# A transformer block with conditioned layer norms: a new token layout and front end, the second norm turned by transposing DMAs, its modulation folded into W1, and new order seeds

## The chip, the cores and the metric

The kernel runs on one core of a Trainium2 chip. A core has a matrix engine (PE, with PEld for its weight loads), a vector engine (DVE), an activation engine (ACT), a general engine (POOL), and a sync engine (SP) that here issues the DMAs. Matrix products land in PSUM, eight banks of 128x512 fp32; everything else lies in SBUF. The metric is the device time of one execution in microseconds (us). Verdicts compare medians of several executions.

## The reference, cut to what matters

One sequence of S = 2048 tokens, D = 512, 32 heads of 16, an MLP of F = 1376, all bf16. The vector `c` gives six modulation vectors of length 512.

```python
mod = (silu(c) @ w_mod).reshape(1, 6, 1, 512)
sa, ca, ga, sb, cb, gb = mod[:, 0], ..., mod[:, 5]
h = layernorm(x) * (1 + ca) + sa
q, k, v = split_heads(h @ wqkv)                 # 32 heads of 16
p = softmax(q @ k.T * 16 ** -0.5)               # no mask
x = x + ga * ((p @ v) @ wo)
h = layernorm(x) * (1 + cb) + sb
x = x + gb * (gelu(h @ w1 + b1) @ w2 + b2)
```

Nothing in it depends on the order of the tokens, as long as queries, residual and output use one order.

## The kernel before, in words

**A planner writes the order.** The function builds operations (`op`, `chain`, `dma`), each with an engine, an assumed duration, dependencies, a priority and perhaps a buffer to acquire (`Res`). `Plan.step` simulates the engines and commits one operation after another; what it commits is emitted at once, so each engine's instruction stream is fixed in the planner's order. An engine runs its stream in order: an instruction that waits holds all that stand behind it. Where several operations could start at about the same time, `Plan.pick` (line 159) takes the lowest of a priority (`dyn`) plus a small number from `Plan.spread` (line 171). That number is a hash of the operation's kind or of its source line, and of a seed from `SEEDS`, one for each 25 us of planned time. A DMA is assumed to land at the time that lines 245 to 248 work out: its issue, 0.75 us, its size at 260 KB a microsecond, and 0.7 us.

```python
q = "SP"
self.bus[q] = max(self.bus[q], s + o.us + 0.75) + o.kb / (300.0 if s < 12.0 else 260.0)
o.end = self.bus[q] + 0.7
```

**Front.** SP loads the first 512 tokens of x in two halves, then two 512 KB pieces of `w_mod` (`load_mod`, line 537). The first 128 columns of Q, K and V weights and the later x blocks wait for the first of these (`behind`, and `o_wm[0]` as a dependency). `mod_columns` (line 620) makes the first norm's shift and scale, `modA`, by 32 one-column matmuls. `layer_norm` (line 666) does the statistics on DVE (`stats`), the reciprocal root on POOL (`rstd`), the normalised z on DVE (`apply`), the transposes on PE into PSUM, and the modulation from PSUM into h on DVE or ACT (`modulate`, line 652). In the first block column groups 0 and 2 go to DVE, 1 and 3 to ACT; groups 0 and 1 lie in one PSUM tile, 2 and 3 in the other. `proj`, `make_q`, `make_k`, `make_v` (lines 732 to 793) make Q, K and V.

**Attention.** 32 runs of one query block of 512 and four heads each; the last query block's runs hold eight heads on half of the queries. A run has 16 key tiles; a tile is 128 keys by 512 queries for four heads, each head a quarter. Quarters take one of two ways:

- ACT way: scores by L853 into PSUM tiles `st` of three or two banks, exponential by ACT (L926), then PV matmuls (L1038) into `od`.
- DVE way: scores by L853 into one of two banks `ax`, L967 turns them into 16-bit integers `ph`, and four shifts (L987 on DVE, the last sometimes in pieces on POOL, L1003) give four bit patterns that are bf16 approximations. All four are multiplied into `od`, so a DVE tile needs four times as many PV matmuls.

Five key tiles of a run may go the DVE way. `next_tile` gives tiles out as the engines come free, and a tile that DVE does not get goes to ACT. The two banks `ax` serve all other products too: projections, transposes of later blocks, `wo`, W1 and W2. Warming matmuls (L479, L463) fill PE's idle time.

At a run's end `normalise` (line 1061) copies `od` to SBUF (L1063) and turns the denominators through small DMAs (L1069 to L1084), and POOL multiplies (L1090). POOL pieces called `beside` run next to DVE instructions that leave the shared port free.

**Block tails.** When a query block is complete, `block_tail` (line 1241) computes `wo`, adds the residual, normalises (the second layer norm, with `modB`), and does W1, gelu, W2 and the store. Its matmuls get due times spread over the following runs, in steps of a fixed length, and each chain takes one or more steps. The transposes of the second norm go by the `else` branch of `layer_norm` (line 707): eight transposes per `ax` bank, then two modulations on DVE. Three tails have four token tiles; the last block's first half has two, and the remaining two token tiles go through `last_half` (line 1312) once all runs are over. `late_loads` fetches the weights after run 0; after run 3 a chain of kind "gate" makes `modB` and the gates `ga`, `gb`. `w2_scaled` folds gb into W2 and `scaled` folds ga into Wo, on POOL.

Of the kernel before, what the change touches and what calls it, by code (L numbers as in the profile page):

```python
# [11 lines left out]
ACT = mybir.ActivationFunctionType  # L12
ALU = mybir.AluOpType
# [41 lines left out]
PEL = 0.24  # L55
# [11 lines left out]
SEEDS = (133, 8, 244, 706, 635, 613, 830, 607, 557, 981, 249, 97, 553, 633, 53, 586, 376, 469, 873, 940, 563, 742, 976, 448, 82, 180, 131, 20, 555, 353, 321, 992)  # L67
# [43 lines left out]
class Plan:  # L111
# [59 lines left out]
    def spread(self, o):  # L171
        x = ((sum(map(ord, o.kind)) if o.eng == "PE" else o.fn.__code__.co_firstlineno if o.fn else 0) * 2654435761 ^ SEEDS[min(int(self.now // 25.0), len(SEEDS) - 1)] * 2246822519) & 0xFFFFFFFF
        x = ((x ^ x >> 15) * 2246822519) & 0xFFFFFFFF
        return SPREAD * ((x ^ x >> 13) & 1023) / 1024.0
# [107 lines left out]
def kernel(  # L282
# [15 lines left out]
    P = 128  # L298
# [187 lines left out]
    x_src = A_x[0].rearrange("(b t p) d -> b p t d", t=TPB, p=P)  # L486
# [12 lines left out]
    qmask = const.tile([P, 2], FP32, name="qmask")  # L499
    Wo = keep.tile([P, NC, D], BF16, name="Wo")  # L500
# [34 lines left out]
    first = {}  # L535

    def load_mod(i):
        def go(o):
            first[i] = nc.sync.dma_start(out=o.tile, in_=wm_src[:, :, i * D:(i + 1) * D])
        return dma(go, kb=512, acq=r_blk, prio=0.01 + 0.01 * i)  # L540
    o_wm = {i: load_mod(i) for i in (0, 1)}

    def behind(i, load):
        tc.add_manual_dep(load.ins, first[i].ins.name, mybir.DependencyInfo(
            mybir.DependencyClass.Sync, mybir.DependencyReason.DATA), reason="order of loads")
# [4 lines left out]
    def load_cols(i, lo, hi, prio):  # L550
        def go(o):
            got = nc.sync.dma_start(out=o_w[i].tile[:, :, lo:hi], in_=wq_src[:, :, i * D + lo:i * D + hi])
            if lo == 0 and i == 0:
                behind(0, got)
# [65 lines left out]
    def mod_columns(dst, ws, kind, warmer=True):  # L620
        mm = chain([(lambda ps, n=n, w=w, m=m: mod_mm(ps, n, w[1](), m, warmer), 0.36 if warmer else 0.22)
# [9 lines left out]
    o_mA = mod_columns(modA, [(o_wm[i], lambda i=i: o_wm[i].tile, o_wm[i]) for i in range(2)],  # L631
# [34 lines left out]
    def layer_norm(src, deps, mod, mod_dep, hold_z, alloc_h, engines, ps_res, kind, prio,  # L666
# [13 lines left out]
        if isinstance(ps_res, tuple):  # L680
            two = []
            for part in range(2):
                for half in range(2):
                    def tr(o, half=half, part=part):
                        if part:
                            o.tile = two[half].tile
                            two[half].ps = o.tile.bitcast(BF16)
                        ps = o.tile.bitcast(BF16)
                        for j in (2 * half, 2 * half + 1):
                            for t in (2 * part, 2 * part + 1):  # L690
                                nc.tensor.transpose(
                                    out=ps[:, (j % 2) * QB + t * P:(j % 2) * QB + (t + 1) * P],
                                    in_=z.tile[:, t, j * P:(j + 1) * P], identity=ident)
                    one = op("PE", tr, 4 * 0.0705, za[0:2 + 2 * part] + [o_id] + two[half:half + part],
                             lat=PEL, mode=("full", 0), kind=kind,
                             acq=None if part else ps_res[half], rel=(z,))
                    one.use = 0.75
                    two.append(one)
            trs += two[2:4]
            for half in range(2):  # L700
                one, done_tr = two[half], two[2 + half]
                for j in (2 * half, 2 * half + 1):
                    e = engines[j]
                    done.append(op(e, lambda o, j=j, e=e, one=one: modulate(
                        e, h.tile[:, j, :], one.ps[:, (j % 2) * QB:(j % 2 + 1) * QB], mod, j),
                        0.5 if e == "DVE" else 0.72, (done_tr, mod_dep, h), prio=0.2, rel=(one,)))
        else:
            N = nt * P
            per = 2 * QB // N
            for j0 in range(0, NC, per):  # L710
                one = chain([(lambda ps, j=j, j0=j0: [nc.tensor.transpose(
                    out=ps.bitcast(BF16)[:, (j - j0) * N + t * P:(j - j0) * N + (t + 1) * P],
                    in_=z.tile[:, t, j * P:(j + 1) * P], identity=ident) for t in range(nt)], nt * 0.0575)
                    for j in range(j0, j0 + per)], za, kind, r_ax, (z,), per)
                trs.append(one)
                for j in range(j0, j0 + per):
                    e = engines[j]
# [823 lines left out]
```

## Time and profile before

| | |
|---|---|
| median of 3 runs | 776.12 us (775.36 to 778.23) |
| profiled execution, its own time | 775.14 us |
| its span | 773.3 us, granted clock 1.000 |
| first exponential starts | 14.66 us |
| last exponential ends | 750.34 us |
| exponentials on ACT (L926) | 623, over 1556 quarter tiles |
| quarter tiles on DVE (L967) | 492 |
| warming matmuls into od (L479) | 41.6 us busy |
| DMA, mean | 36 GB/s |

The span is the time from the first to the last instruction of one profiled execution. Busy times of an engine are unions of its instructions; PE's instructions overlap, and so do DVE's and ACT's at their ends, so that the distance from one start to the next is shorter than the mean duration. A line such as L967 is the place in the kernel that wrote the instruction. After `<-` stands what ended the idle time before it.

### The profile page before, as it was taken

The page shows a single profiled execution, that of the slowest core. Times are in us where ns is not written, and L with a number is a line of the kernel's source. Part 1 is how long each engine was busy: PE and PEld are TensorE (multiplying, and loading weights), DVE is VectorE, ACT ScalarE, POOL GpSimd, SP SyncE. Part 2 cuts the span into 40 slices and gives each one's busy share as a digit, 9 for nine tenths or more (in the row PEclk, how much of TensorE's full clock was granted, in tenths as well). Part 3 has the DMA queues.
Part 4 walks back from the last instruction along what each step waited for, and adds up shares of the span by engine and source line. Part 5 has one row for each costly group of instructions (what it writes and reads, how often), then busy time and mean ns, then how long its engine had stood idle before and what let it go on. Part 6 is the DMA issues. An engine that isn't in the chain of part 4 may idle for free.

```text
span 773.3 us, 20346 instructions
## 1 busy us (share of the span) xinstructions
PE 717.4 (93%) x7984; PEld 264.3 (34%) x8060; DVE 719.7 (93%) x1238; ACT 747.3 (97%) x674; POOL 329.3 (43%) x600
## 2 busy tenths in 40 slices
PE   8999999999999988998999999999999989999998
PEld 3433333333322222223222233232234334334355
DVE  6889789999999999999999988999999999999894
ACT  4999999999999999999999999999999999999994
POOL 6521464444444544654443523333433445243431
PEclk9999999999999999999999999999999999999999
DMA  7142010000300011000100010000110101000100
GB/s 218 35 125 95 25 44 17 26 3 21 78 23 16 27 36 31 19 11 19 44 20 23 23 32 16 21 21 19 31 58 20 30 26 46 17 14 22 32 19 28
DMA packets 38546, 27.69 MB, mean 36 GB/s; under 512 B 17941, under 2 KB 33846, under 8 KB 38450
## 3 DMA queue, kind: packets, MB, share of 16 engines
q1 hardware_dynamic: 38442, 26.39, 11.8%
q8 instruction: 63, 1.03, 0.5%
q14 instruction: 33, 0.27, 0.1%
q10 hardware_dynamic: 8, 0.00, 0.0%
HBM read 20.77 MB, written 2.61 MB: 30 GB/s over the span
## 4 chain that ended last, share of the span: by engine, by line
ACT 46%; PE 28%; issue 13%; DVE 11%; POOL 1%; DMA 0%; SPq 0%; DVEq 0%; POOLq 0%; ACTq 0%
ACT pt L926 45%; PE od L1038 8%; PE st L853 8%; DVE ph L967 4%; PE ax L1211 3%; DVE sh L987 3%; PE ax L853 2%; PE ax L733 1%; PE od L479 1%; PE ax L1271 1%; DVE ln_s L638 1%; PE ax L463 1%; DVE OD L1063 1%; DVE z L649 1%; PE t L1382 1%
## 5 line engine op out<-in xcount | busy, mean ns | idle before, releaser
L926 ACT ACTIVATE pt<-st 128x1536 bf16<-128x1536 f32 x623 | 705.9, 1358 | 2.8 <-PE st L853 1.0
L967 DVE TENSOR_SCALAR ph<-ax 128x512 int16<-128x512 f32 x492 | 322.5, 681 | 26.8 <-PE ax L853 24.9
L1003 POOL TENSOR_SCALAR sg<-ph 128x512 int16<-128x512 int16 x328 | 205.0, 625 | 305.7 <-DVE sh L987 197.9
L987 DVE TENSOR_SCALAR sh<-ph 128x2048 int16<-128x2048 int16 x410 | 280.4, 713 | 2.0 <-PE od L1038 1.0
L853 PE MATMUL st<-qm,kT 32*128 32x512 bf16 x1556 | 243.7, 382 | 32.3 <-ACT pt L926 24.1
L853 PE MATMUL ax<-qm,kT 32*128 32x512 bf16 x492 | 168.6, 379 | 4.5 <-DVE ph L967 2.4
L853 PEld LDWEIGHTS <-kT 32*128 32x128 bf16 x2048 | 83.5, 91 | 245.4 <-issue 234.5
L1038 PE MATMUL od<-pt,VEB 128*32 128x512 bf16 (+1 forms) x1944 | 142.9, 340 | 0.4 <-issue 0.3
L1038 PE MATMUL od<-sh,VX 128*32 128x512 bf16 (+1 forms) x1428 | 106.5, 342 | 2.1 <-DVE sh L987 1.9
L1038 PEld LDWEIGHTS <-VEB 128*32 128x32 bf16 x2560 | 61.5, 96 | 76.2 <-issue 62.5
L1038 PEld LDWEIGHTS <-VX 128*32 128x32 bf16 x1848 | 44.4, 95 | 71.0 <-issue 63.8
L1038 PE MATMUL od<-sh,VEB 128*32 128x512 bf16 (+1 forms) x616 | 48.6, 340 | 2.3 <-DVE OD L1063 2.1
L1090 POOL TENSOR_TENSOR OT<-OD,RB 128x256 bf16<-128x256 f32 x38 | 27.9, 749 | 43.3 <-DVE sh L987 33.2
L1271 PE MATMUL ax<-blk,W 128*128 128x512 bf16 (+1 forms) x157 | 41.8, 353 | 1.5 <-issue 0.5
L479 PE MATMUL od<-warm 128*32 128x512 bf16 x432 | 41.6, 382 | 0.0
L733 PE MATMUL ax<-blk,w 128*128 128x512 bf16 x100 | 32.2, 382 | 2.5 <-issue 0.6
L1211 PE MATMUL ax<-w,g 128*128 128x512 bf16 x113 | 31.7, 381 | 2.0 <-issue 0.8
L1038 PE MATMUL od<-sg,VX 128*32 128x512 bf16 (+1 forms) x420 | 33.3, 338 | 0.0
L1276 DVE TENSOR_SCALAR g<-ax,b1c 128x512 bf16<-128x512 f32 (+1 forms) x44 | 29.1, 673 | 1.1 <-PE ax L1271 1.0
L788 POOL TENSOR_SCALAR VX<-VEB 128x128 bf16<-128x128 bf16 x60 | 20.8, 348 | 20.7 <-DVE VEB L664 17.3
L1090 POOL TENSOR_TENSOR OS<-OD,RB 128x256 bf16<-128x256 f32 x24 | 17.2, 729 | 20.9 <-DVE sh L987 16.4
L638 DVE BATCH_NORM_STATS2 ln_s<-xb 128x6 f32<-128x512 bf16 x32 | 21.6, 675 | 1.4 <-DMA xb<-in_A_x_dram 1.3
(108 smaller groups left out, 411.1 us busy)
## 6 DMA issues: line engine op xcount, KB each, us to landing
RB<-rn SPq DMA_DIRECT2D x124, 64.0 KB, 2.0
xb<-in_A_x_dram SPq DMA_DIRECT2D x7, 512.0 KB
out_dram<-o SPq DMA_DIRECT2D x16, 128.0 KB, 1.8
qm<-qs SPq DMA_DIRECT2D x120, 16.0 KB, 1.8
W<-in_B_w_dram SPq DMA_DIRECT2D x1, 1376.0 KB
w<-in_A_wqkv_dram SPq DMA_DIRECT2D x3, 384.0 KB
blk<-in_w_mod_dram SPq DMA_DIRECT2D x2, 512.0 KB
g<-in_w_mod_dram SPq DMA_DIRECT2D x2, 512.0 KB
```

Of the source, the lines that this page charges most:

```text
L479: nc.tensor.matmul(out=o_od[r].tile[32 * i:32 * i + 32, :], lhsT=warm[:, 0:32], rhs=warm[:, 0:1].to_broadcast([P, QB]), start=False, stop= ...
L638: nc.vector.bn_stats(out=st6, in_=src)
L733: return chain([(lambda ps, j=j: nc.tensor.matmul(out=ps[:, 0:QB], lhsT=w.tile[:, j, cc * P:(cc + 1) * P], rhs=o_h[b].tile[:, j, :], start ...
L853: nc.tensor.matmul(out=o.tile[:, k * QB:(k + 1) * QB], lhsT=kT[cc][kb][rows, ko * P:(ko + 1) * P], rhs=qm.tile[rows, par, :] if hb is None ...
L926: nc.scalar.activation(out=e.tile[:, 0:total * QB], in_=o.tile[:, 0:total * QB], func=ACT.Exp, scale=ESC)
L967: nc.vector.tensor_scalar(out=ph.tile[:, o.row * QB:(o.row + 1) * QB], in0=o.tile, scalar1=PH_B, scalar2=PH_LOW, op0=ALU.add, op1=ALU.max)
L987: nc.vector.tensor_scalar(out=o.tile, in0=first.tile, scalar1=1.0 / FINE, scalar2=PH_0 + PH_SH[j], op0=ALU.mult, op1=ALU.add)
L1003: after_dve(nc.gpsimd.tensor_scalar(out=sh.tile[:, c], in0=first.tile[:, c], scalar1=1.0 / FINE, scalar2=PH_0 + PH_SH[j], op0=ALU.mult, op ...
L1038: nc.tensor.matmul(out=o_od[r].tile[32 * i:32 * i + 32, n * HB:n * HB + w], lhsT=v_tile(kt, ph)[:, c0:c0 + 32], rhs=got[i][:, at:at + w], ...
L1090: two = beside(lambda c: nc.gpsimd.tensor_tensor(out=OT.tile[:, c], in0=OD.tile[:, c], in1=o5.tile[:, c], op=ALU.mult), (OT,), (OD, o5), f ...
L1211: nc.tensor.matmul(out=ps, lhsT=g[:, f, col:col + P], rhs=rhs, start=(f == 0), stop=(f == NF - 1))
L1271: mm = chain([(lambda ps, f=f, j=j, f0=f0: nc.tensor.matmul(out=ps[:, (f - f0) * N:(f - f0 + 1) * N], lhsT=W1[:, j, f * P:(f + 1) * P], rh ...
```

## The change

- Tokens: partition p of a 512-token block holds four neighbouring tokens (`(b p t)`) instead of every 128th (`(b t p)`); loads of x and stores of the output use the same order.
- Front: the two pieces of `w_mod` become one 1 MB load into the g buffer; nothing waits for it any more in SP's queue by an added dependency; in the first block DVE modulates column groups 0 and 1, ACT 2 and 3; projections accumulate in the order 0, 2, 1, 3; the first 128 keys are copied out of PSUM by an instruction of their own.
- Second layer norm in `block_tail`: `norm_turned` writes z, and a transposing DMA on SP per token tile writes h. There is no modulation: `fold_w1` adds `sb @ W1` to b1 (44 one-column matmuls) and multiplies the rows of W1 by `1 + cb` on POOL (12 pieces). In `last_half` PE still transposes, and the modulation becomes a copy.
- The modB pieces of `w_mod` come as one load. The queries of the last runs are asked for one group earlier, and a last-block score waits in the planner for both halves of its queries.
- `SEEDS`: 50 new seeds, one for each 16 us.

```diff
-SEEDS = (133, 8, 244, 706, 635, 613, ...)
+SEEDS = (29, 932, 256, 388, 841, 336, ...)
...
-    ... SEEDS[min(int(self.now // 25.0), len(SEEDS) - 1)] ...
+    ... SEEDS[min(int(self.now // 16.0), len(SEEDS) - 1)] ...
...
-    x_src = A_x[0].rearrange("(b t p) d -> b p t d", t=TPB, p=P)
+    x_src = A_x[0].rearrange("(b p t) d -> b p t d", t=TPB, p=P)
+    out_dst = out[0].rearrange("(b p t) d -> b t p d", t=TPB, p=P)
...
-    o_wm = {i: load_mod(i) for i in (0, 1)}
+    g0 = op("NIL", None, 0.0, (), lat=0.0, prio=-2.0, acq=r_g)
+    def mod_pair(tile_):
+        return tile_[:, 0:2 * NC, :].rearrange("p f q -> p (f q)").rearrange("p (j n) -> p j n", n=2 * D)
+    def mod_part(tile_, n):
+        return mod_pair(tile_)[:, :, n * D:(n + 1) * D]
+    o_wm = dma(lambda o: nc.sync.dma_start(out=mod_pair(g0.tile), in_=wm_src[:, :, 0:2 * D]), (g0,), kb=1024, prio=0.01)
...
-        return dma(go, (o_w[i], o_wm[0]), kb=(hi - lo) * (2 if lo == 0 else 1), prio=prio, n=2.7)
+        return dma(go, (o_w[i],), kb=(hi - lo) * (2 if lo == 0 else 1), prio=prio, n=2.7)
...
-        o_x[b] = load_x(b, (o_wm[0],))
+        o_x[b] = load_x(b)
...
+    def norm_turned(src, deps, nt, prio):
+        ln = op("NIL", None, 0.0, (), lat=0.0, prio=0.0, acq=r_ln)
+        st = [op("DVE", lambda o, t=t: stats(ln, t, src(t)), 0.83, (deps[t], ln), prio=prio) for t in range(nt)]
+        rs = [op("POOL", lambda o, i=i: rstd(ln, 2 * i, 2 * i + 2), 1.3,
+                 st[2 * i:2 * i + 2] + [o_mh], prio=0.0) for i in range(nt // 2)]
+        z = op("NIL", None, 0.0, (rs[0],), lat=0.0, prio=0.0, acq=r_z)
+        h = op("NIL", None, 0.0, (rs[0],), lat=0.0, prio=0.0, acq=r_blk)
+        done = []
+        for t in range(nt):
+            za = op("DVE", lambda o, t=t: apply(ln, z, t, src(t)), 0.33, (z, rs[t // 2]), prio=prio, rel=(ln,), port=True)
+            done.append(dma(lambda o, t=t: nc.sync.dma_start_transpose(
+                out=h.tile[:, :, t * P:(t + 1) * P], in_=z.tile[:, t, :]), (za, h), kb=128, n=2, prio=0.3, rel=(z,)))
+        return h, done
...
     def proj(b, w, cc, kind, acq, after=None):
+        js = (0, 2, 1, 3)
...
+        if (cc, b) == (0, 0):
+            o_k0.append(op(eng, lambda o: copy(eng, kT[cc][b][:, 0:P], mm.tile[:, 0:P]), 0.25, (mm,), prio=0.2, rel=(mm,)))
...
-        want_q(r // 2 + 1 if r < LAST * 8 else r - LAST * 4 + 2)
+        want_q(r // 2 + (1 if r < LAST * 8 - 4 else 2) if r < LAST * 8 else r - LAST * 4 + 3)
...
+    def fold_w1():
+        sb = op("DVE", lambda o: nc.vector.tensor_copy(out=sb_bf, in_=modB[:, 0:NC]), 0.1, (o_late["mB"],), prio=1.0)
+        def column(ps, f):
+            for j in range(NC):
+                nc.tensor.matmul(out=ps[:, f:f + 1], lhsT=W1[:, j, f * P:(f + 1) * P], rhs=sb_bf[:, j:j + 1],
+                                 start=(j == 0), stop=(j == NC - 1))
+        mm = chain([(lambda ps, f=f: column(ps, f), 0.22) for f in range(NF)], [sb, o_late["w1"]], "gate", r_ax, use=0.1)
+        o_late["b1"] = op("DVE", lambda o: nc.vector.tensor_tensor(out=b1c, in0=mm.tile[:, 0:NF], in1=b1_bf, op=ALU.add),
+                          0.15, (mm, o_late["small"]), prio=1.0, rel=(mm,))
+        got = []
+        for j in range(NC):
+            for lo in range(0, NF * P, QB):
+                c = slice(lo, min(lo + QB, NF * P))
+                got.append(op("POOL", lambda o, j=j, c=c: after_dve(nc.gpsimd.tensor_scalar(
+                    out=W1[:, j, c], in0=W1[:, j, c], scalar1=modB[:, NC + j:NC + j + 1], scalar2=0.0,
+                    op0=ALU.mult, op1=ALU.add)), G_US, (mm, o_late["mB"]), lat=0.1, prio=2.0, kind="beside", port=True,
+                    gate=lambda: plan.beside(G_MIN)))
+        o_late["w1"] = op("NIL", None, 0.0, got, lat=0.0, prio=0.0)
...
-        h, hd, za, trs = layer_norm(lambda t: x2.tile[:, t, :], res_done, modB, o_late["mB"],
-                                    None, r_blk, ("DVE",) * 4, r_ax, kind, 0.3, None, nt)
+        h, hd = norm_turned(lambda t: x2.tile[:, t, :], res_done, nt, 0.3)
...
-                    hd.append(op(e, lambda o, n=n, j=j, e=e, at=at, tro=tro: modulate(
+                    hd.append(op(e, lambda o, n=n, j=j, e=e, at=at, tro=tro: copy(
...
-            ("DVE", "ACT") * 2 if b == 0 else ("DVE", "DVE", "ACT", "ACT") if b < 3 else ("DVE",) * 4, ...
+            ("DVE", "DVE", "ACT", "ACT") if b < 3 else ("DVE",) * 4, ...
```

More of the change, by code (lines that the diff above doesn't have):

```diff
@@ L630, in mod_columns @@
         return op("DVE", out_, 0.4, (mm,), prio=0.65, rel=(mm,))
-    o_mA = mod_columns(modA, [(o_wm[i], lambda i=i: o_wm[i].tile, o_wm[i]) for i in range(2)],
+    o_mA = mod_columns(modA, [(o_wm, lambda i=i: mod_part(g0.tile, i), g0) for i in range(2)],
                        "modA", False)
@@ L679, in layer_norm @@
         trs = []
[L680 to L699, printed above, removed]
-            for half in range(2):
[L701 to L717, printed above, removed]
-                    done.append(op(e, lambda o, j=j, j0=j0, one=one, e=e: modulate(
-                        e, h.tile[:, j, 0:N], one.tile.bitcast(BF16)[:, (j - j0) * N:(j - j0 + 1) * N], mod, j),
-                        0.1 + nt * 0.09, (one, mod_dep, h), prio=0.1, rel=(one,)))
@@ new lines, in layer_norm @@
+        trs += two[2:4]
+        for half in range(2):
+            one, done_tr = two[half], two[2 + half]
+            for j in (2 * half, 2 * half + 1):
+                e = engines[j]
+                done.append(op(e, lambda o, j=j, e=e, one=one: modulate(
+                    e, h.tile[:, j, :], one.ps[:, (j % 2) * QB:(j % 2 + 1) * QB], mod, j),
+                    0.5 if e == "DVE" else 0.72, (done_tr, mod_dep, h), prio=0.2, rel=(one,)))
+        return h, done, za, trs
+    def norm_turned(src, deps, nt, prio):
[11 more added lines that the diff above has]
+        return h, done
@@ L1309, in store @@
         dma(lambda o: nc.sync.dma_start(
[L1310 removed]
+            out=out_dst[b, t], in_=a.tile), (a,), kb=128, rel=(a,))
     def last_half():
@@ L1489 @@
                 o_late["mB"] = mod_columns(
-                    modB, [(o_late[3 + n], lambda n=n: gt.tile[:, 4 * n:4 * n + 4, :], gt)
-                           for n in range(2)], "gate")
+                    modB, [(o_late[3], lambda n=n: mod_part(gt.tile, n), gt) for n in range(2)], "gate")
+                fold_w1()
                 o_late[5] = load_w(wm_src[:, :, 5 * D:6 * D], r_xb, (o_late["ga"],), prio=5.0)
```

61 lines of the change are left out of this document (31 added, 30 removed).

## The prediction

> **What bounds the kernel now.** I read the page's busy line first, then the windows (busy time of each engine in 25 us stretches), the groups by form, the waits, and the timelines of the front and of the tail.
>
> The page's first lines; each engine's busy time, share of the span, instructions.
>
> ```profile
> span 773.3 us, 20346 instructions
> PE 717.4 (93%) x7984; PEld 264.3 (34%) x8060; DVE 719.7 (93%) x1238; ACT 747.3 (97%) x674; POOL 329.3 (43%) x600
> ```
>
> The windows: length, then busy time and instructions of PE, PEld, DVE, ACT, POOL.
>
> ```profile
> 90.00:115.00 25.00, 23.62 (x246) 9.09 (x247) 19.13 (x31) 25.00 (x24) 14.40 (x28) 1.00 0.12 37
> ...
> 290.00:315.00 25.00, 22.72 (x251) 7.28 (x250) 24.81 (x42) 25.00 (x24) 11.75 (x18) 1.00 0.09 25
> ...
> 440.00:465.00 25.00, 23.91 (x232) 7.55 (x235) 21.80 (x38) 24.88 (x23) 7.04 (x11) 1.00 0.13 36
> ```
>
> ACT is full in every stretch: over 40 to 740 us its idle time sums to 1.9 us. So between the first exponential (14.66 us) and the end of the last (750.34 us) only less ACT work helps. Score tiles are shared out between ACT and DVE as each comes free, so time won on DVE turns into tiles that ACT need not do. DVE is uneven: 24.8 in one stretch, 19.1 and 21.8 in others.
>
> Groups by form: line, engine, operation, shapes, count, then busy us, mean ns, and idle time before them.
>
> ```profile
> L967 DVE TENSOR_SCALAR ph<-ax 128x512 int16<-128x512 f32 x492 | 322.5, 681 | 26.8 <-PE ax L853 24.9
> L987 DVE TENSOR_SCALAR sh<-ph 128x2048 int16<-128x2048 int16 x410 | 280.4, 713 | 2.0 <-PE od L1038 1.0
> L657 DVE TENSOR_SCALAR blk<-ax,modB 128x512 bf16<-128x512 bf16 x12 | 6.0, 531 | 0.0
> L657 DVE TENSOR_SCALAR blk<-ax,modB 128x256 bf16<-128x256 bf16 x4 | 1.4, 398 | 0.0
> L711 PE MATMUL ax<-ident,z 128*128 128x128 bf16 x56 | 4.5, 220 | 0.0
> ```
>
> The reader sees DVE's idle time ended by PE, which writes DVE's scores into the two ax banks (24.9 us), and the 16 modulations and 56 transposes that go.
>
> Timelines of the front and of the pitch: start, length, engine, line, count, what ended the idle time before.
>
> ```profile
> 9.18 0.47 PEld L614 LDWEIGHTS <-blk 128*128 128x128 bf16 x16 [0.34 <-DMA blk<-in_w_mod_dram]
> ...
> 10.47 0.99 DVE L657 TENSOR_SCALAR blk<-st,modA 128x512 bf16<-128x512 bf16 x2 [0.29 <-PE st L691]
> ...
> 11.05 1.45 ACT L654 ACTIVATE blk<-st,modA 128x512 bf16<-128x512 bf16 x2 [3.09 <-DVE blk L657]
> ...
> 13.37 1.41 DVE L751 TENSOR_SCALAR qm<-st,qmask 128x512 bf16<-128x512 f32 x2 [1.91 <-PE st L733]
> ...
> 13.59 0.59 ACT L662 CAST kT<-ax 128x512 bf16<-128x512 f32 x1 [1.09 <-PE ax L733]
> ...
> 103.15 1.89 DVE L967 TENSOR_SCALAR ph<-ax 128x512 int16<-128x512 f32 x3 [0.17 <-PE ax L853]
> ```
>
> The second half of w_mod is waited for at 9.18; ACT's modulation starts only when DVE's first is over; three L967 in 1.89 us are a pitch of 0.60 us.
>
> **The rate of exchange.** Between 14.66 and 750.34 lie 735.7 us, of which about 27.0 are other ACT work (three gelus 14.7, six table loads 7.6, three kT casts 1.8, four modulations 2.9). The other 708.7 us do 1556 quarter tiles: 0.455 us each. A quarter on DVE is one L967 and 410/492 of an L987, both at the 0.60 us pitch: 1.10 us. Moving n quarters for x us of DVE shortens both engines alike: n = x / (0.455 + 1.10), so the time falls by 0.29 x.
>
> **The change, part by part.** The profiled execution took 775.14 us (span 773.3 and 1.84 around it), 0.98 below the median of 776.12. The sum is made against the profiled one and carried to the median.
>
> 1. *Second layer norm, removed.* Twelve modulations at a pitch of 0.46 (two take 0.99 with a mean of 0.53) are 5.5 us of DVE, four half ones at 0.33 are 1.3: 6.8 us, times 0.29 = **-2.0**. The 56 transposes (16 take 1.05 us in the front, so about 3.7 us) free PE time that is worth nothing by itself: PE fills 41.6 us with warming matmuls at L479. Bounds: 0 if no whole tile moves, -3.6 if two tiles (eight quarters) do.
>
> 2. *Second layer norm, added.* Fourteen transposing DMAs of 128 KB on SP. No row shows one. The nearest is the 128 KB store of the output, 1.8 us to landing; the far row is a 512 KB load, 4.6. The planner assumes 1.24 us of issue each and a landing 3.2 us after the start (lines 245 to 248 with n=2), the last of four 6.9 us after the first. I take the near row: **0**, covered by the planner's 3.2. The cover matters because PE runs in order: the first W1 matmuls (L1271) are placed where h is believed landed, and both score streams queue behind them. With the transposes gone the due times pull L1271 forward (transposes stood at 354.9 and 363.9, L1271 at 367.8), so little slack is left. On SP the next denominators (L1069 to L1084) and mask copies (L761) queue behind. Runs end 23.2 us apart (OD copies at 567.72 and 590.91), RB is issued 8 us after a copy and OD has two buffers: some 15 us to spare. Bounds 0 to +35 (rival C).
>
> 3. *Folding into W1.* 44 one-column matmuls, 16 of which take 0.55 us: 1.5 us of PE, but the chain of 11 pieces holds one of the two ax banks about as long as the eight pieces of modB did (118.8 to 123.4), say 5.5 us. At worst L967 then runs at half pitch: 2.7 us of DVE, +0.8; at best 0. The twelve POOL pieces of 0.63 (row L1003) meet a POOL that is 43% busy; if each displaced a quarter of an L987, 12 x 0.15 x 0.29 = +0.5. I take **+0.3** for both, nearer to no cost, because around the modB pieces DVE waited 0.4 us only.
>
> 4. *Front.* With DVE on j 0 and 1 and ACT on 2 and 3, ACT need not wait for DVE in one bank: it starts 0.58 earlier. In block 1, which has that split, the two start together (21.97 and 22.04). Copying 128 keys first saves at most 0.1, since qm's first half ends about 14.08, and its second copy costs ACT 0.2. Against that, one w_mod DMA in place of two makes all 32 columns wait for its end: 16 more x 0.034 = +0.55, less the 0.3 that modA was early. Loads sent at once instead of after w_mod's first half: w landed at 10.83, not last, so 0. Together **-0.2**; bounds -1.2 (w_mod by 8.2) to +0.8 (half a us later).
>
> 5. *Tail.* The last modulations become copies; the chain has one on each of two token tiles (338 ns on DVE). **-0.1**, bounds -0.4 to 0. The layout of the loads and stores changes only descriptors; x is waited for at the first tile alone: 0. Queries of the last block are made one group earlier; PE waited 0.2 us on a qm: 0.
>
> 6. *Order.* New seeds, drawn every 16 us, and no chains of the second norm in ax. Over the 28 stretches from 40 to 740 DVE is idle 31.5 us; the median stretch is 24.36 busy, and 18.2 us lie in stretches below it. If all came up to the median: -5.3. An unlucky order can lose as much: +5.3. I take half the gain, 9.1 x 0.29 = **-2.7**: stretches with the same kinds of work, block tails among them (290 to 415), already reach 24.6 to 24.8, and the worst ones are those where projections and gate chains crowd the two banks.
>
> Sum: -2.0 + 0 + 0.3 - 0.2 - 0.1 - 2.7 = -4.7. From 775.14 to 770.4, at the median **771.4 us**. About 0.5% (3.9 us) is what a measurement of this kernel can tell from no change.
>
> On part 2 the Trainium skill has two rules that no run here shows. "VectorE: DVE Perf Modes", section The three transpose paths, gives 1309 ns for a 128x128 transpose by DMA against 390 ns on TensorE: an estimate from it is 5.2 us per 128x512 and 21 us for four in a row, 14 us later than planned, which by rival C's working would cost over 40 us. "Advanced Engine Details and Errata", section X-Bar Transpose (TRN2), calls such DMAs as fast as ordinary ones, which would leave the sum as it is.
>
> **Rivals.**
> B, *the order gives nothing.* Parts 1 to 5 alone are -2.0: 774.1. For it: PE is 93% busy and each tile moved to DVE needs three more rounds of PV matmuls; the waits on L853 may be PE's order, not the banks. Against it: the warming matmuls that would make room. With part 6 from -1.9 to +5.3 this case spans 772.3 to 779.4.
> C, *the transposes land late and stop PE.* Place: L1271 behind hd in three full blocks and a half one. If the four go one after the other at T each, the last lands 4T after issue instead of 6.9. Rows for T: 2.6 (128 KB of w columns) to 4.6 (512 KB). ACT has one further filled score tile, 1.1 us, as a cushion. T = 3.6: late 7.5, so 3 x 6.4 + 1.7 in the half block = +21: 792. At 2.6 it is +7.2, at 4.6 +35. It decides the sign of a measurable change from T = 2.7 on (3 x (4T - 8.0) = 8.6). For it: a late copy already stopped DVE once (dc waiting for dn, 1.1 us). Against it: 1.8 us for stores of this size, which overlap.
>
> **How the numbers follow.** A (forecast, order gains more than 1.9): 0.56, 771.4, its own range 764 to 772.2, the low end being all 31.5 us of DVE idle time won (-9.2) with the front's -1.2. B: 0.28. C: 0.16. A and B hold 0.84; I cut B's last bit and take 764 to 779. Faster 0.56, within 0.5% 0.28, slower 0.16.
>
> **What would show it.** Right: L967 near 502 and exponentials near 619 instead of 623; first exponential at 14.4; stretches 90 to 115 and 440 to 465 above 23 on DVE; no idle time of PE ended by a DMA at L1271; the tail after the last exponential still about 23 us. Wrong: L967 still 492 (B); L1271 or its weight loads waiting on a DMA into h (C); modA later than 10.7 with the first exponential after 14.7 (front). The forecast fails most easily by part 6, whose sign no row fixes.

## The result, and the profile after

The changed kernel takes **774.29 us** (median; 772.62 to 775.25) against 776.1 for the kernel before in the same comparison. The ratio is 0.9971, with a 95% interval from 0.9958 to 0.9985: 0.3% faster, 1.8 us, less than the 0.5% that counts as told from no change. Forecast were 4.7 us less. The time is that of rival B (774.1), not that of the forecast (771.4).

The changed kernel's profiled execution took 774.01 us. The first lines of its page; each engine's busy time, share of the span, instructions:

```profile
span 772.1 us, 20489 instructions
PE 726.5 (94%) x8066; PEld 263.9 (34%) x8066; DVE 718.5 (93%) x1233; ACT 744.8 (96%) x673; POOL 333.9 (43%) x604
```

ACT has 2.5 us less to do than before (747.3), and still fills the span. The exponentials on ACT and DVE's two groups for its tiles, with busy us, mean ns, and idle time before them:

```profile
L926 ACT ACTIVATE pt<-st 128x1536 bf16<-128x1536 f32 (+1 forms) x621 | 704.4, 1350 | 3.7 <-PE ax L853 2.3
L967 DVE TENSOR_SCALAR ph<-ax 128x512 int16<-128x512 f32 x496 | 325.1, 681 | 23.1 <-PE ax L853 20.6
L987 DVE TENSOR_SCALAR sh<-ph 128x2048 int16<-128x2048 int16 x416 | 285.0, 715 | 1.9 <-PE od L1038 1.0
```

DVE does 496 quarter tiles instead of 492, that is one whole tile more, and ACT 621 exponentials instead of 623. The forecast had 502 and 619. DVE still waits 20.6 us in front of L967 for PE's scores (24.9 before).

Two windows of the kernel before that the prediction does not show (length; busy time and instructions of PE, PEld, DVE, ACT, POOL; PE's granted clock; DMA share and GB/s):

```profile
140.00:165.00 25.00, 23.27 (x249) 8.26 (x249) 25.00 (x43) 24.97 (x23) 10.44 (x19) 1.00 0.06 18
165.00:190.00 25.00, 23.08 (x252) 9.01 (x255) 24.50 (x41) 25.00 (x23) 12.22 (x25) 1.00 0.06 16
```

And the windows of the changed kernel:

```profile
90.00:115.00 25.00, 23.49 (x241) 7.76 (x233) 22.98 (x39) 25.00 (x23) 10.90 (x18) 1.00 0.15 42
140.00:165.00 25.00, 22.63 (x273) 8.43 (x269) 20.92 (x37) 24.89 (x23) 14.12 (x23) 0.95 0.07 19
165.00:190.00 25.00, 24.45 (x268) 9.26 (x264) 23.35 (x40) 24.11 (x23) 13.67 (x27) 0.98 0.06 16
...
440.00:465.00 25.00, 23.65 (x219) 6.93 (x216) 24.35 (x45) 24.97 (x23) 12.66 (x20) 1.00 0.23 45
```

The two stretches that were named as poor got better: DVE is busy 22.98 instead of 19.13 at 90 to 115, and 24.35 instead of 21.80 at 440 to 465. But 140 to 190, where the kernel before had 25.0 and 24.5, now has 20.92 and 23.35, and there the clock column is below 1.00. Over all 28 stretches from 40 to 740, DVE's idle time went from 31.5 to 27.5 us, and ACT's from 1.9 to 3.0.

The spans cut at the first and last exponential say where the time went. The column for E1 (an experiment below, in which the clock stays at 1.000) belongs to the changed kernel too:

| us | before | after | difference | E1 | difference |
|---|---|---|---|---|---|
| front, to the first exponential | 14.66 | 15.28 | +0.62 | 15.18 | +0.52 |
| first exponential to the end of the last | 735.68 | 734.31 | -1.37 | 733.52 | -2.16 |
| tail after it | 22.96 | 22.51 | -0.45 | 22.50 | -0.46 |
| span | 773.3 | 772.1 | -1.2 | 771.2 | -2.1 |

The middle of that table as one window each, of the kernel before, of the changed kernel and of E1:

```profile
14.66:750.34 735.68, 685.47 (x7701) 246.53 (x7773) 700.00 (x1190) 732.14 (x639) 316.56 (x552) 1.00 0.11 33
15.28:749.59 734.31, 693.85 (x7802) 246.31 (x7802) 699.53 (x1186) 730.40 (x637) 321.26 (x557) 1.00 0.12 34
15.18:748.70 733.52, 694.36 (x7813) 246.55 (x7812) 698.87 (x1186) 730.42 (x637) 318.88 (x557) 1.00 0.13 34
```

Length less busy time is what DVE idles there: 35.7 us before, 34.8 after, 34.7 in E1. Where ACT is full, then, DVE won only 1.0 us of idle time. The 4.0 us of the 28 stretches say more than that, because they leave out the ends of the middle, where the changed kernel idles more.

Three things have to be explained: why the middle gained 1.4 and not some 4.4, why the front got longer, and what happens at 160 us.

### The profile page after: what moved, and what is told of

It reads as the page before. It is cut to its first block, busy times and chain, and to the rows that moved or that the text cites. A ratio compares the mean times of both kernels' runs of the same rounds, so it can differ in the third digit from the quotient of the medians.

```text
span 772.1 us, 20489 instructions
## 1 busy us (share of the span) xinstructions
PE 726.5 (94%) x8066; PEld 263.9 (34%) x8066; DVE 718.5 (93%) x1233; ACT 744.8 (96%) x673; POOL 333.9 (43%) x604
## 3 DMA queue, kind: packets, MB, share of 16 engines
q8 instruction: 63, 1.03, 0.6%
## 5 line engine op out<-in xcount | busy, mean ns | idle before, releaser
L926 ACT ACTIVATE pt<-st 128x1536 bf16<-128x1536 f32 (+1 forms) x621 | 704.4, 1350 | 3.7 <-PE ax L853 2.3
L967 DVE TENSOR_SCALAR ph<-ax 128x512 int16<-128x512 f32 x496 | 325.1, 681 | 23.1 <-PE ax L853 20.6
L1003 POOL TENSOR_SCALAR sg<-ph 128x512 int16<-128x512 int16 x320 | 199.8, 624 | 293.3 <-DVE sh L987 186.5
L987 DVE TENSOR_SCALAR sh<-ph 128x2048 int16<-128x2048 int16 x416 | 285.0, 715 | 1.9 <-PE od L1038 1.0
L853 PE MATMUL ax<-qm,kT 32*128 32x512 bf16 x496 | 170.4, 380 | 3.7 <-DVE ph L967 2.2
L853 PEld LDWEIGHTS <-kT 32*128 32x128 bf16 x2048 | 85.6, 91 | 250.1 <-issue 240.7
L1038 PE MATMUL od<-sh,VX 128*32 128x512 bf16 (+1 forms) x1464 | 110.5, 342 | 1.1 <-DVE sh L987 0.7
L1284 PE MATMUL ax<-blk,W 128*128 128x512 bf16 (+1 forms) x176 | 43.6, 355 | 0.4 <-DVE ph L967 0.4
L730 PE MATMUL ax<-blk,w 128*128 128x512 bf16 x124 | 35.9, 382 | 0.5 <-ACT blk L651 0.2
L1225 PE MATMUL ax<-w,g 128*128 128x512 bf16 x128 | 34.4, 381 | 0.9 <-ACT g L1294 0.6
L635 DVE BATCH_NORM_STATS2 ln_s<-xb 128x6 f32<-128x512 bf16 x32 | 21.7, 677 | 1.4 <-DMA xb<-in_A_x_dram 1.4
```

What stands on the lines that cost most here:

```text
L730: return chain([(lambda ps, j=j: nc.tensor.matmul(out=ps[:, 0:QB], lhsT=w.tile[:, j, cc * P:(cc + 1) * P], rhs=o_h[b].tile[:, j, :], start ...
L853: nc.tensor.matmul(out=o.tile[:, k * QB:(k + 1) * QB], lhsT=kT[cc][kb][rows, ko * P:(ko + 1) * P], rhs=qm.tile[rows, par, :] if hb is None ...
L926: nc.scalar.activation(out=e.tile[:, 0:total * QB], in_=o.tile[:, 0:total * QB], func=ACT.Exp, scale=ESC)
L967: nc.vector.tensor_scalar(out=ph.tile[:, o.row * QB:(o.row + 1) * QB], in0=o.tile, scalar1=PH_B, scalar2=PH_LOW, op0=ALU.add, op1=ALU.max)
L987: nc.vector.tensor_scalar(out=o.tile, in0=first.tile, scalar1=1.0 / FINE, scalar2=PH_0 + PH_SH[j], op0=ALU.mult, op1=ALU.add)
L1003: after_dve(nc.gpsimd.tensor_scalar(out=sh.tile[:, c], in0=first.tile[:, c], scalar1=1.0 / FINE, scalar2=PH_0 + PH_SH[j], op0=ALU.mult, op ...
```

## The experiments

In E1 to E6 and E9 to E11 every instruction stays in the changed kernel's order; only what an operation emits is altered.

**E1, warming matmuls among the fold's columns.** The clock at 160 us, in the changed kernel's own trace. First PE's timeline (start, length, line, shape, count):

```profile
159.16 0.65 PE L1187 MATMUL ax<-sb_bf,W 128*128 128x1 bf16 x20
...
162.01 0.39 PE L853 MATMUL st<-qm,kT 32*128 32x512 bf16 x2 [0.44 <-ACT pt L926]
...
163.61 0.61 PE L853 MATMUL st<-qm,kT 32*128 32x512 bf16 x3
```

The same score matmul takes 0.39 us at 162.01 and 0.61 at 163.61: the clock fell between the two, in the middle of `fold_w1`'s 44 one-column matmuls (156.9 to 164.4). The windows around it:

```profile
157.00:160.00 3.00, 2.56 (x52) 1.52 (x52) 2.99 (x5) 3.00 (x4) 1.35 (x2) 1.00 0.00 0
160.00:163.00 3.00, 2.43 (x29) 0.72 (x26) 1.38 (x2) 3.00 (x4) 2.63 (x5) 0.95 0.02 5
163.00:166.00 3.00, 3.00 (x36) 0.93 (x28) 2.19 (x5) 2.67 (x3) 0.73 (x2) 0.50 0.01 3
166.00:169.00 3.00, 3.00 (x43) 0.95 (x39) 2.78 (x5) 2.33 (x3) 1.38 (x3) 0.98 0.03 3
```

For 3.4 us (162.7 to 166.1) the granted clock is 0.50, behind 6 us in which PE was busy 5.0. E1 adds to each of the eleven pieces one wide matmul into the unused columns of the same bank:

```diff
-                nc.tensor.matmul(out=ps[:, f:f + 1], ..., start=(j == 0), stop=(j == NC - 1))
+                nc.tensor.matmul(out=ps[:, f:f + 1], ..., start=(j == 0), stop=(j == NC - 1))
+            nc.tensor.matmul(out=ps[:, P:QB], lhsT=warm, start=True, stop=True, rhs=warm[:, 0:1].to_broadcast([P, QB - P]))
```

> The changed kernel with one warming matmul of 384 columns behind each of the 11 pieces of the fold's column matmuls, every other instruction in the same order. Theory (the one-column matmuls leave the array too idle, the granted clock falls to 0.5 for some 3.5 us near 163 us, and that costs 1.5 to 2 us in most executions): clock 1.000, about 772.7 us, ratio to before about 0.9957. Rival (the order around 160 us has the gap anyway, from the waits of L853 on L926): the clock still falls, 774 to 775 us. Rival (the extra 1.8 us of PE work matters): slower than 774.5.

Measured: 773.49 us (773.05 to 773.74), ratio 0.9965 (0.9952 to 0.9978) to the kernel before. The same windows in E1:

```profile
157.00:160.00 3.00, 3.00 (x50) 1.55 (x47) 2.87 (x5) 3.00 (x4) 1.46 (x2) 1.00 0.02 5
160.00:163.00 3.00, 3.00 (x40) 1.04 (x38) 1.38 (x2) 2.87 (x3) 1.95 (x4) 1.00 0.00 0
163.00:166.00 3.00, 3.00 (x49) 1.11 (x41) 2.57 (x5) 2.93 (x4) 1.29 (x2) 1.00 0.01 3
166.00:169.00 3.00, 3.00 (x38) 0.91 (x37) 3.00 (x6) 3.00 (x4) 2.02 (x4) 1.00 0.05 8
```

The clock stays at 1.00, and the mean clock was 0.999 or 1.000 in all seven executions of E1. So wide work among the fold's narrow matmuls removes the dip. By time alone E1 is not told from the result (0.9965 against 0.9971); the clock is what it shows. It does not show that the narrow matmuls alone make the dip: E1 fills whatever gap there is, also that of the scores' waits on ACT (0.44 us at 162.01), which was the rival. PE's busy share alone does not decide either. In the changed kernel's own trace PE is busy 4.68 us of the 6 from 334 to 340, and the clock stays at 1.00:

```profile
334.00:337.00 3.00, 2.69 (x32) 0.91 (x31) 3.00 (x7) 3.00 (x4) 0.00 (x0) 1.00 0.00 0
337.00:340.00 3.00, 2.00 (x25) 0.61 (x21) 2.96 (x7) 2.96 (x4) 1.90 (x4) 1.00 0.34 67
```

And in E7 (below), where the same 44 matmuls stand in another order (145.5 to 153.7), the clock stays at 1.00 too. The dip takes the chain and the stretch it lies in together; what in them sets it off stays open. What stays without the dip is DVE's 1.38 us of 3.00 at 160 to 163: that gap is not the clock's. ACT, full at 166 to 169 in E1, has 2.33 of 3.00 in the changed kernel: the bill of the dip comes when the score banks have run empty.

**E2, w_mod's first columns by two loads again.**

```diff
-    o_wm = dma(lambda o: nc.sync.dma_start(out=mod_pair(g0.tile), in_=wm_src[:, :, 0:2 * D]), (g0,), kb=1024, prio=0.01)
+    o_wm = dma(lambda o: [first.append(nc.sync.dma_start(out=mod_part(g0.tile, n), in_=wm_src[:, :, n * D:(n + 1) * D])) for n in range(2)], (g0,), kb=1024, prio=0.01)
```

The front of the changed kernel, in its timeline:

```profile
9.81 0.87 PEld L611 LDWEIGHTS <-g 128*128 128x128 bf16 x32 [0.34 <-DMA g<-in_w_mod_dram]
...
10.81 0.17 DVE L624 COPY modA<-ax 128x8 f32<-128x8 f32 x1 [1.73 <-PE ax L611]
...
11.50 0.99 DVE L654 TENSOR_SCALAR blk<-st,modA 128x512 bf16<-128x512 bf16 x2 [0.23 <-PE st L687]
...
11.72 1.45 ACT L651 ACTIVATE blk<-st,modA 128x512 bf16<-128x512 bf16 x2 [4.04 <-PE st L687]
...
15.28 1.45 ACT L926 ACTIVATE pt<-st 128x1536 bf16<-128x1536 f32 x1 [0.38 <-PE st L853]
```

w_mod is waited for until 9.81 (9.18 before), and modA comes at 10.81 (9.78 before). ACT starts 0.22 us after DVE instead of 0.58, as was said.

> The changed kernel with w_mod's first 1024 columns as two 512 KB DMAs one behind the other, nothing else moved. Theory (the single landing makes all 32 columns wait): the first 16 columns start near 8.5, the last 16 near 9.8, modA is ready by 10.6 instead of 11.3, the first exponential at 14.7 instead of 15.28. Rival (w_mod lands late because the loads sent right behind it share its queue): both halves land after 9.5 and the first exponential stays near 15.2.

Measured: modA at 9.98 and the first exponential at 14.62, 0.66 us earlier; 774.5 us with a mean clock of 0.995. By itself this reads as a cure. It is not one: E5, E6, E10 and E11 load w_mod in the same way, and their first exponentials start at 15.22, 14.78, 15.81 and 14.87. With E2 the mean is 15.06; the five profiles with one load (the changed kernel, E1, E4, and, described below, E9 and, with other seeds, E7) have 15.28, 15.18, 15.03, 14.96 and 15.07, mean 15.10. Two loads scatter more, and no gain is shown.

**E3, two loads, and the first weight columns wait for the first of them**, as in the kernel before:

```diff
-            nc.sync.dma_start(out=o_w[i].tile[:, :, lo:hi], ...)
+            got = nc.sync.dma_start(out=o_w[i].tile[:, :, lo:hi], ...); (lo == 0 and i == 0) and tc.add_manual_dep(got.ins, first[0].ins.name, ..., reason="order of loads")
```

> As the run with two loads, and the first 128 columns of the weights (and with them everything behind in SP's queue) wait until the first half of w_mod has landed, as in the kernel before. Theory (the traffic behind w_mod delays it): second half lands near 9.2, the first exponential at 14.1 to 14.3, earlier than before's 14.66 because DVE and ACT modulate side by side. Rival (single landing only): no gain over the run with two loads alone, or a loss because the weights arrive after 10.8.

Measured: 776.43 us, clock 0.993, first exponential at 15.86. E3's timeline:

```profile
13.82 0.69 DVE L635 BATCH_NORM_STATS2 ln_s<-xb 128x6 f32<-128x512 bf16 x1 [1.80 <-DMA xb<-in_A_x_dram]
...
15.42 0.39 PE L853 MATMUL st<-qm,kT 32*128 32x512 bf16 x3 [1.20 <-DVE qm L751]
```

The weights' wait also holds the next block's x on SP's queue, and in this order DVE does that block's statistics (L635) ahead of the masks of the first queries (L751). The first scores wait 1.20 us for those. In this one profile a wait put back alone, without the order that went with it, cost more than it saved; the clock fell to 0.50 twice in it as well, near 20 and at 161 to 168.

**E4, each transposing DMA issued twice into the same place.**

```diff
-            done.append(dma(lambda o, t=t: nc.sync.dma_start_transpose(
-                out=h.tile[:, :, t * P:(t + 1) * P], in_=z.tile[:, t, :]), ...
+            done.append(dma(lambda o, t=t: [nc.sync.dma_start_transpose(
+                out=h.tile[:, :, t * P:(t + 1) * P], in_=z.tile[:, t, :]) for _ in range(2)], ...
```

> The changed kernel with each of the 14 transposing DMAs issued twice into the same place; the second must wait for the first to land, which shows the landing time on SP. Theory (hidden, lands in about 2 us): SP's second issue waits about 2 us, W1's matmuls L1284 wait little, time within 1.5 us of the changed kernel's. Rival C of the prediction (PE in order behind late transposes): with twice the DMAs PE waits several us at L1284 in each block, time 780 us or more.

In the changed kernel the last two of the first block's four transposes, and the first W1 matmul, stand like this on the timeline:

```profile
343.06 1.20 SPq L716 DMA_TRANSPOSE blk<-z  x1
...
346.45 1.02 PE L1284 MATMUL ax<-blk,W 128*128 128x512 bf16 x4
```

No wait on a DMA stands in front of L1284 (line 1271 before). In E4 the timeline has:

```profile
349.91 1.19 SPq L716 DMA_TRANSPOSE blk<-z  x1
...
356.78 1.87 PE L1284 MATMUL ax<-blk,W 128*128 128x512 bf16 x4 [9.38 <-DMA blk<-z]
...
359.29 1.02 ACT L926 ACTIVATE pt<-st 128x1024 bf16<-128x1024 f32 x1 [10.12 <-PE st L853]
```

and PE's waits in E4 (us in total, times, longest):

```profile
PE ax L1284 <- DMA blk<-z: 13.7, 2, 9.4
PE ax L853 <- DMA qm<-qs: 8.5, 1, 8.5
```

and one of SP's own:

```profile
SPq L716 <- DMA blk<-z: 18.3, 14, 2.7
```

Measured: 805.54 us, 31 more than the changed kernel, with a mean clock of 0.972. The first of the pair shown was issued at 347.48 (its issue takes 1.19), and SP, after a wait on a semaphore, started the second, which writes the same place, at 349.91. I read that as a landing of the first no more than 2.43 us after the start of the issue. Of the 14 pairs 13 stand 2.43 to 2.73 us apart, and one 4.01. The planner assumes 3.2, which covers all but that one; in the changed kernel, which issues each once, no wait of PE on them shows. When they come late, PE stops, both score streams stop behind it, and ACT idles 10 us: rival C's mechanism is real and dear. 22.2 us of the 31 are PE's waits in these two lines, the second through SP's queue (L761 behind the transposes); the clock falls to 0.50 in each of PE's three waits and stays there behind them, at 349 to 363, 479 to 493 and 653 to 663, and at the fold as well (162 to 168).

**E5 and E6, warming and two loads together**, in E5 with all eleven warming matmuls, in E6 with every second one:

```diff
+            f % 2 == 1 and nc.tensor.matmul(out=ps[:, P:QB], lhsT=warm, start=True, stop=True, rhs=warm[:, 0:1].to_broadcast([P, QB - P]))
```

> The changed kernel with both repairs, the order untouched: a 384-column warming matmul behind each of the fold's 11 pieces, and w_mod's first 1024 columns as two loads. Theory (each repair gives its own gain and they add): clock 1.000, first exponential at 14.6, about 772.8 us (773.5 with the warming alone, less 0.66). Rival (a gain in the front is absorbed later): 773.5.

> As the run before, with the warming matmul behind every second piece only. Theory (the clock needs some array work in each stretch of a few microseconds, and each further warming matmul only costs 0.16 us of PE time): clock 1.000 and 0.3 to 0.8 us faster than with all eleven. Rival (half is not enough): the clock falls in some executions, 773 to 775 us.

Measured: E5 773.13 us (772.61 to 773.54), ratio 0.9960 (0.9946 to 0.9973); E6 772.29 us (771.55 to 772.79), ratio 0.9948 (0.9935 to 0.9962). The clock was 0.999 or 1.000 in all executions of both. E6 is 0.8 below E5. In their profiles 0.4 of that lies ahead of the first exponential (14.78 against 15.22), where neither has a warming matmul of the fold; so at most 0.4 is the price of the six further matmuls, and that is not shown by one profile each. Five kept the clock up in the stretch at 160.

**E7 and E8, the changed kernel and the kernel before with seeds drawn at random, nothing else altered.** The planner settles each order, and with it the split of the tiles, before anything runs, so the tiles can be counted in the program as it is emitted. In 20 programs of each kind with random seeds, DVE gets 478.2 quarters on average in the kernel before (standard deviation 3.8, at most 484), 482.8 in the changed kernel (5.0, at most 492), and 478.0 in the changed kernel with the second norm turned on PE as before. The kernels' own seeds give 492 and 496. These are counts of programs, not of runs; the four that ran agree with their traces (L967). For the chip one program of each kind with 480 quarters was taken.

```diff
-SEEDS = (29, 932, 256, 388, ...)      # E7; E8: (133, 8, 244, 706, ...)
+SEEDS = (600, 22, 371, 822, ...)      # E7; E8: (654, 129, 319, 85, ...)
```

> The changed kernel with seeds drawn at random. It gives DVE 480 quarter tiles instead of 496. Theory (the seeds were worth 16 quarters of 0.455 us to the changed kernel): 774.3 + 7.3 = 781.6 us, 780 to 784. Rival (the tiles that DVE gets say little about the time): within 2 us of 774.3.

> The kernel before with seeds drawn at random. It gives DVE 480 quarter tiles instead of 492. Theory (both kernels' seeds were worth about as much, so choosing them anew gave nothing net): 776.1 + 5.5 = 781.6 us, 780 to 784, and the difference between this run and the changed kernel with random seeds is small for equal tile counts. Rival (the seeds of before were worth less than those of the changed kernel): 778 or less.

Measured: E7 789.54 us, 1.0178 of the kernel before (1.0156 to 1.0199); E8 791.06 us, 1.0191 (1.0173 to 1.0209). E7's group of L967:

```profile
L967 DVE TENSOR_SCALAR ph<-ax 128x512 int16<-128x512 f32 x480 | 315.1, 681 | 28.9 <-PE ax L853 26.7 <-PE st L853 0.4
```

By spans the chosen seeds are worth 14.3 us in the changed kernel (786.4 against 772.1) and 16.1 in the kernel before (789.4 against 773.3). At 0.455 us a quarter, 16 and 12 quarters would be 7.3 and 5.5; the orders are worth more than their tiles. DVE idles 55.1 and 54.5 us between 40 and 740, ACT 8.3 and 4.8. In E7 all of the loss lies between the exponentials (748.9 instead of 734.3); in E8 8.5 us do, 3.7 lie in the front (another order of the loads) and 3.9 in the tail. With unpicked seeds the changed kernel is 1.5 us ahead, with picked ones 1.8, which looks as if new seeds against old ones had given nothing. But this is one draw each: 4 to 5 quarters of standard deviation are some 2 us, and the times differ by more than the tiles. Between the exponentials alone, where the prediction had put the gain of the order, the draws cost the changed kernel 14.6 us and the kernel before 8.5. So the two runs show that both kernels' seeds are picked and dear to lose; that the new seeds are worth no more than the old ones rests on the counts (+13 and +14 quarters over the mean of random ones) and on DVE's idle time in the middle.

**E9, E10, E11: the changed kernel again, E6 again, and E6 with three warming matmuls** (`f % 4 == 1`), in one comparison with 18 executions of the kernel before (median 775.8).

> The changed kernel as it is, beside the two repaired versions on one chip. Theory (clock drop at the fold in most executions, late w_mod in the front): 774.3 us median, some executions near 772.7 at clock 1.000, the others 774 to 775.3 at 0.995 to 0.998.

> Two loads in the front and a warming matmul behind every second piece of the fold, once more beside the changed kernel. Theory: 772.3 us, 1.5 to 2.5 us below the changed kernel, clock 0.999 or 1.000 in every execution. Rival (the gain seen before lay between chips): within 1 us of the changed kernel.

> As the run before, with a warming matmul behind three of the eleven pieces only. Theory (three are too far apart to keep the clock): clock below 0.999 in some executions, 772.5 to 774.5. Rival (any interruption of the one-column stretch is enough): 772.0.

Measured: E9 774.73 us (772.82 to 777.56), ratio 0.9988 (0.9978 to 0.9997); E10 773.52 (771.96 to 774.48), 0.9965 (0.9952 to 0.9978); E11 773.16 (772.55 to 774.98), 0.9968 (0.9957 to 0.9980). So the changed kernel's gain is 0.1 to 0.3%, and E10 with its five matmuls is another 0.2% faster. E11's profile has the dip at 162 (clock 0.50) and one at 340, so three did not always keep the clock up there; but three of its six executions have a clock of 1.000, and by its median it is as fast as E10. The times do not tell five from three. E10's windows at 160 are at 1.00, yet another place dips:

```profile
205.00:208.00 3.00, 2.57 (x22) 0.72 (x17) 2.92 (x6) 3.00 (x4) 1.67 (x3) 1.00 0.00 0
208.00:211.00 3.00, 3.00 (x27) 0.60 (x25) 2.54 (x5) 2.35 (x3) 1.29 (x3) 0.53 0.06 11
211.00:214.00 3.00, 3.00 (x25) 0.74 (x24) 2.17 (x4) 2.70 (x3) 1.31 (x2) 0.90 0.00 0
```

No fold is near. In half of E10's executions the mean clock is 0.997 and the time 774.4 to 774.5; in the others it is 0.999 or 1.000 and the time 772.0 to 772.7. The fold is thus the commonest place of a dip in these profiles, not the only one: E9 has a further one at 667, and E7 (260) and E8 (355), with random seeds, have one each in stretches of ordinary matmuls, E8 without any fold. Over the executions in the comparisons of the result and of E1 to E11, as far as their clock is on record:

| | mean clock 0.999 or more | their median | lower clock | their median |
|---|---|---|---|---|
| before | 25 | 775.57 | 16 | 776.70 |
| changed (result and E9) | 3 | 772.82 | 17 | 774.80 |
| E1, E5, E6, E10 together | 22 | - | 3 | 774.46 |
| E11 | 3 | 772.64 | 3 | 774.29 |

At a full clock the change is worth 2.75 us. If lower clocks are the whole difference between the columns, they cost the kernel before 16/41 x 1.13 = 0.4 us on average and the changed kernel 17/20 x 1.98 = 1.7: it gives some 1.2 of the 2.75 back. The first of these numbers rests on three executions, but E1, which differs by the warming alone, has 2.1 by spans and 2.5 by medians (773.49 against 775.95).

**E12, the kernel before, profiled a second time**, for its front.

> The kernel before, unchanged, profiled a second time, to learn how firm the start of its first exponential is. In the profile that the forecast was made from it stood at 14.66 us; the five profiles of the changed kernel with one load of w_mod have 14.96 to 15.28, the five with two loads 14.62 to 15.81. Theory L, the layout's loads make the front later: the kernel before again has its first exponential at 14.5 to 14.8. Theory S, the landing of the first loads scatters from execution to execution by more than the layouts differ: it lies anywhere between 14.4 and 15.8, and no difference of a few tenths in the front can be given to the change.

```profile
9.84 0.17 DVE L627 COPY modA<-ax 128x8 f32<-128x8 f32 x1 [0.78 <-PE ax L614]
...
14.73 1.45 ACT L926 ACTIVATE pt<-st 128x1536 bf16<-128x1536 f32 x1 [0.49 <-PE st L853]
```

Measured: 775.48 us; modA at 9.84 and the first exponential at 14.73, against 9.78 and 14.66 in the first profile. Those 0.07 apart and the five one-load profiles at 14.96 to 15.28 do not overlap: as far as two profiles and five can tell, the front did get later, by 0.2 to 0.6 us.

## Why the prediction was wrong

**Part 6, the order (-2.7): the step that failed.** It reasoned that DVE's idle time below the median stretch is there to be won, and that new seeds win half of it, 9.1 us. Between the exponentials 1.0 us was won (35.7 to 34.7 in E1), which at 0.29 is 0.3 us instead of 2.7 (over the 28 stretches from 40 to 740 alone 4.0, or 1.2 us). The stretches named were won (+3.9 and +2.6 us of DVE), but 140 to 190 lost most of that: even in E1, at a full clock, they have 21.06 and 23.67 busy, 4.8 us less than before. 2.2 of these 4.8 can be put to the fold's held bank (part 3); without them the order would have won 3.2 us of DVE, or 0.9. What the newly chosen order filled in two places it opened in another, and by the counts the old order was as well chosen as the new one (+14 and +13 quarters over random ones). By these measures the term was worth 0.3 to 1.2, nearer to rival B's 0 than to 2.7, and 0 stood within the bounds of +/-5.3.

**Part 1, the second norm removed (-2.0): right**, as far as the parts can be told apart. One whole tile moved, four quarters, where 6.8/1.555 = 4.4 follow from the sum; four times 0.455 are 1.8 us. Four more of L967 and six more of L987, at the pitch of 0.60, take 6.0 of the 6.8 us that DVE was freed of. In the counts of unpicked orders, turning the norm alone gives 4.8. Exponentials fell by 1.5 us of busy time.

**Part 2, the transposing DMAs (0): right**, and for the reason given: by E4 they land within 2.4 to 2.7 us but for one of 4.0, nearer to the 1.8 of the store than to the 4.6 of the 512 KB load. Rival C was to decide from 2.7 on. The margin is small, and E4 shows what late ones cost: 31 us.

The estimate of 5.2 us per 128x512 from the Trainium skill's "VectorE: DVE Perf Modes", section The three transpose paths, is twice what was measured. The Trainium skill's "Advanced Engine Details and Errata", section X-Bar Transpose (TRN2), which calls them as fast as ordinary DMAs, fits the trace: 2.4 to 2.7 us against 2.6 for 128 KB of weight columns.

**Part 3, folding into W1 (+0.3): a term was missed.** It priced PE time, the held bank and POOL, and had nothing for the granted clock. That fell to 0.50 at this place in all six profiles in this order without warming or with three matmuls, for 3.4 us in the changed kernel and E11 and for 6.8 in E2, E3, E4 and E9, and in none of the four with five or eleven. With the dips elsewhere it is 1.2 us on average. The rows that the fold was priced from, those of modB in the kernel before, hide the risk: there each four one-column matmuls are followed by a wide one, and the clock stays at 1.00.

```profile
L617 PE MATMUL ax<-warm 128*128 128x384 bf16 x8 | 2.4, 322 | 0.0
```

The chain held its bank for 7.5 us, not 5.5, and that seems to cost besides: in E1, where only the clock is mended, DVE has 7.8 us busy of 10 in 155 to 165, where the kernel before had all 10; 2.2 at 0.29 are 0.6. And two of the shifts came back from POOL to DVE: the four further quarters need four, and L987 rose by six; 2 x 0.60 x 0.29 = 0.3, though that the fold's pieces pushed them out is not shown. Bank and POOL lie within their bounds of 0.8 and 0.5; the 1.2 of the clock come on top.

The Trainium skill's "TensorE: Matmul & The Clock Gate", Part 1: The HAM clock gate, has the half clock after an idle window of about 3.4 us. The trace agrees on the half (0.50); but PE was not idle, it shows 5.0 busy of the 6 us before.

**Part 4, the front (-0.2): wrong sign**, within the bounds (-1.2 to +0.8). The gain from the split between DVE and ACT came: from modA to the first exponential it takes 4.47 us instead of 4.88. The loads were mis-sized. "Loads sent at once: 0" was argued from w, which is not last, but what they slow is w_mod: it lands at 9.81 instead of 9.18 with everything in flight, and with the 32 columns behind one end modA is 1.03 later, not 0.25. Whether the one load or the loss of the waits does more was not separated: E2 and its likes scatter too much.

**Part 5, the tail (-0.1):** -0.45, a little past the bound of -0.4; why was not looked into.

**The sum**, at a full clock by E1's trace: front +0.5, middle -2.2, tail -0.5, together -2.1. The middle was forecast at -4.4. Of the difference of 2.2 part 6 is 1.8 (-0.9 instead of -2.7) and bank and POOL of part 3 some 0.6 (+0.9 instead of +0.3); the sizes are too rough for the rest. The dips take another 1.2 on average.

## What to carry to other kernels

A gain that a new order is to bring over a chosen one is worth 0 until its tiles are counted in the program: the idle time that a trace shows below its median stretch is not there to be won for free, as here two fills went with a gap elsewhere. Measure what was won over the whole stretch in which the limiting engine is full, here from the first to the last exponential, and not in windows at fixed times. On a PE kept at full clock by its load, price an added chain of narrow matmuls by what it does to the granted clock in its stretch, and give it a few wide ones from the start, as the chain of modB had. A front's forecast needs two profiles of the same kernel, because loads that are sent together scatter by more than the tenths that are to be won.

## What was not expected of the hardware

- The granted clock fell to 0.50 while the profile shows PE 83% busy in the 6 us before, and not behind 6 us at 78% in the same trace; five wide matmuls among 44 narrow ones prevented it there. Lighter stretches elsewhere dip in some executions and not in others (208 us in E10, 667 in E9).
- The dips last 3.4 us or about a multiple of it: 3.4 in the changed kernel, 6.8 at the same place in E9, 10.2 and 13.7 at the waits of E4.
- Transposing a 128x512 bf16 tile from SBUF to SBUF by DMA takes 1.2 us of SP's issue and landed within 2.4 to 2.7 us of its start in 13 of 14 pairs of E4, within 4.0 in the other.
- One load of 1 MB, sent with the other loads, is waited for until 9.6 to 9.9 us; the first columns behind two loads of 512 KB started at 9.0 to 10.4.
